# Layer A attention with the exponents stationary and a column of ones beside the values

## The chip, the cores and the metric

The kernel runs on one core of a Trainium2 chip. The metric is the device time of one launch in microseconds (us), given as the median of several runs. The core has a matrix engine (TensorE, PE in the profile; PEld are its weight loads), VectorE (DVE), ScalarE (ACT), GpSimd (POOL) and SyncE (SP), which here only issues DMAs. Sixteen DMA engines move all data between DRAM and the on-chip memory. Matmuls write to a memory called PSUM in the code.

## The reference

Four layers follow each other, A, B, A, B, each added to its input and fed by a layernorm without weights. Layer B is a linear attention over the whole sequence and is not touched by the change, apart from a step at its start that completes the output of layer A. Layer A is a recurrence over 64 segments:

```python
B, S, Dm = 1, 2048, 640;  H, Dh = 32, 192;  M, seg = 8, 32
mask = (idx[:, None] < M) | (idx[:, None] >= idx[None, :])
mem = mem0                                            # 8 rows
for s in range(64):
    h = concatenate([mem, xs], axis=1)                # 8 + 32 rows of 640
    q, k, v = h @ Wq, h @ Wk, h @ Wv                  # 32 heads of 192
    p = softmax(where(mask, q @ k.T * Dh ** -0.5, -1e9))
    o = (p @ v) @ Wo                                  # 40 rows of 640
    mem = o[:, :M];  outs.append(o[:, M:])
```

A segment needs the eight memory rows that the segment before it puts out, so the 64 segments run one after the other. All weights of layer A (Wq, Wk, Wv, Wo, 7.86 MB each in bfloat16) pass through the array in every segment.

## The kernel before

**Preparation (`A_pre`).** The last eight rows of each segment influence nothing in the recurrence. Their queries, keys and values ("tails") are made for all segments at once and stored in DRAM (`kqb_d`, `vb_d`). In the first layer this stage also lays out two of the four parts of Wo in DRAM (`lay_out_wo`, `wo_rows`), so that a later load of them has rows of 2560 bytes; the other two parts are loaded from Wo itself.

**The chain (`A_chain`).** A segment handles the other 32 rows: eight of memory, 24 of input. Its transposed rows `hT` are the stationary operand, 32 columns wide; four matmuls stand side by side in the array's four column groups (`tile_position=(0, 32 * g)`), each with 384 columns of weights moving. The 32 heads are split into four rounds of eight. For one round:

- `q_or_k` and `project` (line 988) make Q and K, 20 matmuls each; `to_raw` (line 998) copies them out on ScalarE, `to_rows` (lines 1003 to 1008) transposes them in 32x32 blocks on VectorE into `QT` and `KT`. V is projected likewise and copied into `Vp` by `v_rows` (lines 1017 and 1019).
- `next_kq` (lines 959 to 967) puts the tails of Q and K beside them and fetches the next ones, `extra_v` (line 971) fetches the tails of V. All this is on GpSimd and its DMA queue. `Vp` lies on partitions 0 to 79; its other partitions hold the input rows that `hx_transpose` (line 943) reads.
- `weigh`: `scores` puts a mask (line 1025) and six products (line 1030) into one bank, 80 keys on the partitions, 320 columns of queries; ScalarE exponentiates it into `E` (line 1085).
- `sums` (line 1099) multiplies `E` by a block of ones, so that each row of the bank holds the sums of the columns; `normalise` makes their inverse with Ln and Exp on ScalarE (lines 1104 and 1105) and VectorE multiplies `E` by it (line 1106).
- `attend` (line 1038) has the values stationary and `E` moving: eight matmuls of 80 columns. Its output is transposed as `wo_round` needs it and is copied into `OT` (lines 1044 and 1045); the tails go to `otb` (`keep_tail`, lines 1051 to 1054) and to DRAM (`store_tail`, line 1058).
- `wo_round` (line 1067), 48 matmuls of 160 columns, adds the round to the segment's output `W`. After the last round VectorE transposes the memory rows of `W` into the next `hT` (lines 1220 and 1221), which the next segment's first projection waits for, and ScalarE copies the output rows out (`keep_rows`, line 951).

The order on each engine is the program's own (`tc.manual_schedule()`), so each engine meets its instructions as they are written. `keep_busy` (line 1074) and `fill` (line 1080) issue matmuls and weight loads whose results nobody reads.

**Weights.** Not all weights fit on the chip. Three of the five pieces of Q, K and V of two rounds share slots: a slot is loaded anew in each segment (`load_slot`, line 681, on SP's queue) once the first round's projection has read it. The order of rounds turns round in every other segment. In the same way the parts 0 and 3 of Wo share `wo_end`; `load_wo` (line 698) loads the one that the last round needs, in six pieces, after `wo_round` of the first. With the tails' small transfers a segment moves 6.09 MB.

**After the chain** `post_steps` (lines 1260 and 1261, in layer B's stage) multiplies the tails' attention by Wo for 16 segments at a time; `spread_tails` orders them for it.

## Time and profile before

| | |
|---|---|
| runs | 3598.80, 3600.39, 3607.37 us; median 3600.39 |
| span of the profiled execution | 3590.5 us, 168460 instructions |
| between the span and the median | 9.9 us |
| busy in the span | PE 97%, DVE 65%, ACT 57%, POOL 44% |
| DMA | 929.38 MB, mean 259 GB/s |
| preparation, first layer | 0 to 181 us |
| chains | 181 to 1540 us and 1980 to 3340 us |
| the remainder of layer B and the second preparation | 1540 to 1980 us and 3340 to 3590 us |
| one segment of a chain | 21.0 us (median) |

The profile is one execution under the hardware profiler. Its span runs from the first to the last instruction, and the runs' times hold some work around it. "Busy" is the union of an engine's instruction times; a matmul's time holds the way through the array, so that PE can be busy all the time without being full. In lists of instructions the bracket at the end of a row tells how long the engine was idle before it and what ended that.

### The profile page before, as it was taken

How to read it: one execution, taken by the hardware profiler on the slowest of the kernel's cores; microseconds unless marked ns; L12 is line 12 of the kernel's file. 1: busy time of each engine (PE TensorE's matmuls, PEld its weight loads, DVE VectorE, ACT ScalarE, POOL GpSimd, SP SyncE). 2: the span in 40 equal slices, each digit the busy share in tenths (PEclk: the TensorE clock that was granted, in tenths of full speed). 3: DMA queues.
4: the chain of work that ended last, by engine and by line, in shares of the span. 5: the costliest groups of instructions: out<-in, count | busy, mean ns of one | idle time of the engine just before them, and what ended most of it. 6: DMA issues, size and time to landing. Idle time of an engine off the chain costs nothing.

```text
span 3590.5 us, 168460 instructions
## 1 busy us (share of the span) xinstructions
PE 3465.5 (97%) x70978; PEld 2268.6 (63%) x71399; DVE 2327.0 (65%) x6320; ACT 2032.0 (57%) x5233; POOL 1589.1 (44%) x4173
## 2 busy tenths in 40 slices
PE   9989999999999999999999899999999999999999
PEld 7756666666666666655377566666666666666553
DVE  5466666667666666746633566666666666676465
ACT  3356666666566656646432556666666666666463
POOL 3445555555555555530123455555545555555400
PEclk9999999999999999999999999999999999999999
DMA  8988888888788878860476878887888888888600
GB/s 311 334 290 288 281 295 282 278 292 299 278 284 295 289 277 278 295 224 3 146 272 217 290 275 287 290 291 278 285 294 279 290 282 292 292 281 287 222 1 30
DMA packets 452689, 929.38 MB, mean 259 GB/s; under 512 B 75338, under 2 KB 218330, under 8 KB 448858
## 3 DMA queue, kind: packets, MB, share of 16 engines
q1 hardware_dynamic: 382266, 817.56, 64.0%
q0 software_dynamic: 67744, 87.80, 7.9%
q8 instruction: 557, 9.13, 1.0%
q10 hardware_dynamic: 1920, 13.24, 0.9%
q14 instruction: 202, 1.65, 0.1%
HBM read 848.50 MB, written 73.73 MB: 257 GB/s over the span
## 4 chain that ended last, share of the span: by engine, by line
PE 55%; DMA 20%; issue 9%; DVE 7%; POOL 5%; ACT 4%; SPq 1%; PEld 0%; POOLq 0%; ACTq 0%; DVEq 0%
PE ps_qk L988 17%; DMA arena<-wo_rows 7%; DMA Vp<-vb 6%; PE ps_v L988 6%; PE ps_w L1067 6%; PE ps_pre L878 3%; PE ps_o L1038 3%; PE ps_s L1030 3%; DVE hT L943 2%; PE ps_s L1099 2%; DMA arena<-in_A_Wv_dram 2%; PE ps_s L1025 2%; PE ps_pre L902 2%; PE ps_idle L1074 2%; PE kv L1260 1%
## 5 line engine op out<-in xcount | busy, mean ns | idle before, releaser
L988 PEld LDWEIGHTS <-hT 128*32 128x32 bf16 x30720 | 746.5, 96 | 431.9 <-DVE hT L1221 27.2
L988 PE MATMUL ps_qk<-arena,hT 128*32 128x384 bf16 x20480 | 998.8, 328 | 14.6 <-DMA arena<-in_A_Wq_dram 4.2
L998 ACT ACTIVATE raw<-ps_qk 128x384 bf16<-128x384 f32 x1024 | 502.0, 490 | 383.7 <-PE ps_s L1099 250.9
L988 PE MATMUL ps_v<-arena,hT 128*32 128x384 bf16 x10240 | 534.6, 328 | 8.7 <-DMA arena<-in_A_Wv_dram 8.4
L971 POOL DMA_DIRECT2D Vp<-vb x512 | 258.4, 505 | 611.4 <-PE ps_o L1038 465.6
L1067 PE MATMUL ps_w<-arena,OT 128*32 128x160 bf16 x18432 | 446.1, 234 | 11.4 <-DMA arena<-wo_rows 10.4
L1003 DVE STREAM_TRANSPOSE KT<-raw 128x384 bf16<-128x384 bf16 x512 | 296.0, 578 | 194.5 <-ACT raw L998 190.5
L1067 PEld LDWEIGHTS <-OT 128*32 128x32 bf16 x18432 | 322.7, 96 | 103.8 <-ACT OT L1044 22.3
L1006 DVE STREAM_TRANSPOSE QT<-raw 128x256 bf16<-128x256 bf16 x512 | 227.9, 445 | 237.5 <-ACT raw L998 195.5
L959 POOL DMA_DIRECT2D kqb<-kqb x512 | 290.9, 568 | 168.9 <-POOL KT L967 147.3
L1019 DVE CAST Vp<-ps_v 64x384 bf16<-64x384 f32 x512 | 286.2, 559 | 113.6 <-ACT Vp L1017 90.0
L1106 DVE TENSOR_TENSOR E<-E,ps_s 80x320 bf16<-80x320 bf16 x512 | 247.4, 483 | 142.7 <-ACT ps_s L1105 142.3
L1058 POOL DMA_DIRECT2D otb<-otb x512 | 282.7, 552 | 128.1 <-DVE otb L1054 100.0
L1017 ACT ACTIVATE Vp<-ps_v 64x384 bf16<-64x384 f32 x512 | 246.1, 481 | 138.4 <-PE ps_v L988 122.9
L1038 PEld LDWEIGHTS <-Vp 80*128 80x128 bf16 x4096 | 189.9, 99 | 123.1 <-issue 80.5
L1038 PE MATMUL ps_o<-E,Vp 80*128 80x80 bf16 x4096 | 233.0, 201 | 31.8 <-DMA Vp<-vb 15.0
L1085 ACT ACTIVATE E<-ps_s 80x320 bf16<-80x320 f32 x512 | 221.4, 432 | 68.0 <-PE ps_s L1030 33.6
L951 ACT ACTIVATE Vp<-ps_w 32x160 bf16<-32x160 f32 x512 | 150.3, 294 | 155.1 <-DVE wt L1220 138.4
L964 POOL COPY QT<-kqb 128x64 bf16<-128x64 bf16 x512 | 124.5, 243 | 254.8 <-PE ps_s L1030 248.5
L1030 PE MATMUL ps_s<-QT,KT 128*80 128x80 bf16 (+1 forms) x3072 | 233.2, 213 | 1.6 <-POOL KT L967 1.5
L1104 ACT ACTIVATE ps_s<-ps_s 80x320 f32<-80x320 f32 x512 | 214.7, 419 | 31.2 <-PE ps_s L1099 31.2
L1030 PEld LDWEIGHTS <-KT 128*80 128x80 bf16 x3072 | 205.4, 119 | 28.7 <-issue 18.3
(156 smaller groups left out, 5446.4 us busy)
## 6 DMA issues: line engine op xcount, KB each, us to landing
arena<-wo_rows SPq DMA_DIRECT2D x780, 320.0 KB, 6.8
arena<-in_A_Wq_dram SPq DMA_DIRECT2D x427, 384.0 KB, 4.4
arena<-in_A_Wv_dram SPq DMA_DIRECT2D x427, 384.0 KB, 6.6
arena<-in_A_Wk_dram SPq DMA_DIRECT2D x768, 192.0 KB, 4.6
kqb<-kqb POOLq DMA_DIRECT2D x512, 48.0 KB, 5.1
arena<-in_A_Wk_dram SPq DMA_DIRECT2D x43, 384.0 KB, 7.8
vb<-arena POOLq DMA_DIRECT2D x128, 112.0 KB, 6.3
Vp<-vb POOLq DMA_DIRECT2D x512, 28.0 KB, 4.8
```

The costliest lines, as they stand in the source:

```text
L959: nc.gpsimd.dma_start(out=kqb[:], in_=self.kqb_d[r, :, s, :])
L971: nc.gpsimd.dma_start(out=Vs[n % 2][64:80, :], in_=self.vb_d[s, r].rearrange("g t f -> (g t) f"))
L988: nc.tensor.matmul(o[32 * g:32 * g + 32, 0:384], lhsT=hT[:, b, :], rhs=rhs, start=(i == 0), stop=(i == KC - 1), tile_position=(0, 32 * g), ...
L998: nc.scalar.activation(out=raw[:], in_=ps[:, 0:384], func=ACT.Copy)
L1003: nc.vector.transpose(out=KT[:, :, 0:64], in_=raw[:, :].rearrange("p (c j) -> p c j", j=64))
L1017: nc.scalar.activation(out=o, in_=i, func=ACT.Copy)
L1019: nc.vector.tensor_copy(out=o, in_=i)
L1030: nc.tensor.matmul(S[0:80, c0:c0 + 80 * (q1 - q0)], lhsT=KT[:, 3 * x + i, :], rhs=QT[:, x, q0:q1, :], start=False, stop=(x == 1 and i == 2 ...
L1038: nc.tensor.matmul(O[x][:, 80 * i:80 * i + 80], lhsT=Vs[n % 2][0:80, 448 * x + k:448 * x + k + 128], rhs=E[0:80, 160 * x + 80 * e:160 * x ...
L1058: nc.gpsimd.dma_start(out=self.otb_d[:, s, 96 * r:96 * r + 96], in_=otb[:, :, :].rearrange("p c t -> p (c t)"))
L1067: nc.tensor.matmul(W[32 * g:32 * g + 32, 0:160], lhsT=OT[:, c, q:q + 32], rhs=w[:, 640 * i + 160 * g:640 * i + 160 * g + 160], start=(firs ...
L1106: nc.vector.tensor_tensor(out=E[0:80, 0:320], in0=E[0:80, 0:320], in1=rc, op=ALU.mult)
```

## The change

Queries, not keys, come out on the partitions. `attend` now has `E` stationary, 32 columns of queries of one head pair at a time in one of the four column groups, and the values moving: 192 columns and one more that holds ones (`VH = 194` is the pitch). So column 192 of the output holds the softmax sum of its row. `sums`, `normalise` and the block of ones go. The output is scaled by the sum's reciprocal where it leaves PSUM (`weigh_rows`, `scaled`) and then transposed in 32x32 blocks on VectorE (`turn`). The tails of two rounds share one bank (`pair`) and are scaled, transposed and stored together. The order of the rows of Wo changes with that, so all four parts are laid out in DRAM, in 32 DMAs. The steps of a round move: `attend` follows the projection of the next K in the same turn of the loop, and the output rounds are cut and placed anew. Of the matmuls that nobody reads (`keep_busy`, 14 in a segment) one of 512 columns is left; `FILL` and `SEG_FILL` are other numbers.

```diff
-FILL = {0: 86, 2: 79}
-SEG_FILL = 2
+FILL = {0: 65, 2: 79}
+SEG_FILL = 1
+
+VH = 194
...
-        self.vb_d = dram.tile([NSEG, NR, 2, 8, 896], BF16, name=f"vb{li}")
+        self.vb_d = dram.tile([NSEG, NR, 2, 8, 4 * VH], BF16, name=f"vb{li}")
...
+                load = nc.sync.dma_start(out=tk, in_=self.wo_rows[r, :, 1280 * k:1280 * k + 1280])
...
+            self.wo_rows = dram.tile([4, P, 7680], BF16, name="wo_rows")
+
+        def lay_out_wo(r):
+            for h in range(4):
+                for G in range(2):
+                    nc.sync.dma_start(out=self.wo_rows[r, 32 * h:32 * h + 32, 3840 * G:3840 * G + 3840]
+                                      .rearrange("f (j m) -> f j m", m=640), in_=wov[8 * r + 4 * G + h])
...
-                        lay_out_wo(ri - 1)
+                        for r1 in (2 * ri - 2, 2 * ri - 1):
+                            lay_out_wo(r1)
...
-            def attend(E, n, OT=None):
-                O = [pop.tile([P, 512], F32, name=f"ps_o{x}", tag=f"o{x}") for x in range(2)]
-                for x in range(2):
-                    for k, e, i in ((0, 0, 0), (320, 1, 2), (128, 0, 1), (192, 1, 1)):
-                        nc.tensor.matmul(O[x][:, 80 * i:80 * i + 80], lhsT=Vs[n % 2][0:80, 448 * x + k:448 * x + k + 128],
-                                         rhs=E[0:80, 160 * x + 80 * e:160 * x + 80 * e + 80], start=(k == 0),
-                                         stop=(k == 192), skip_group_check=True)
-                if OT is None:
-                    OT = sp.tile([P, 6, 64], BF16, name="OT", tag="OT")
-                o = [x[:, 0:240].rearrange("p (i q) -> p i q", q=80) for x in O]
-                nc.scalar.activation(out=OT[:, 0:3, :], in_=o[0][:, :, 0:64], func=ACT.Copy)
-                nc.vector.tensor_copy(out=OT[:, 3:6, :], in_=o[1][:, :, 0:64])
-                return OT, o
-
...
+            pair = [None]
+
+            def attend(E, n):
+                O = pop.tile([P, 512], F32, name="ps_o", tag="o0")
+                V = Vs[n % 2]
+                for G in range(2):
+                    for h in range(4):
+                        nc.tensor.matmul(O[32 * h:32 * h + 32, VH * G:VH * G + 193], lhsT=E[0:80, 80 * h + 32 * G:80 * h + 32 * G + 32],
+                                         rhs=V[0:80, VH * h:VH * h + 193], start=True, stop=True, tile_position=(0, 32 * h),
+                                         skip_group_check=True)
+                if n % 2 == 0:
+                    pair[0] = pop.tile([P, 512], F32, name="ps_t", tag="o1")
+                q, m = (48, 32) if n % 2 == 0 else (64, 16)
+                for h in range(4):
+                    nc.tensor.matmul(pair[0][32 * h:32 * h + m, 0:193], lhsT=E[0:80, 80 * h + q:80 * h + q + m],
+                                     rhs=V[0:80, VH * h:VH * h + 193], start=True, stop=True, tile_position=(0, 32 * h),
+                                     skip_group_check=True)
+                return O
+
+            def weigh_rows(O):
+                rc = sp.tile([P, 2], F32, name="rc", tag="rc")
+                nc.vector.reciprocal(out=rc[:], in_=O[:, 0:2 * VH].rearrange("p (g f) -> p g f", f=VH)[:, :, 192])
+                return rc
+
+            def scaled(out, O, rc, G, eng):
+                i = O[:, VH * G:VH * G + 192]
+                if eng == "s":
+                    nc.scalar.activation(out=out, in_=i, func=ACT.Copy, scale=rc[:, G:G + 1])
                 else:
-                    nc.scalar.activation(out=otb[:, 0:3, :], in_=o[0][:, :, 64:80], func=ACT.Copy)
-                self.chain_end = [nc.vector.tensor_copy(out=otb[:, 3:6, :], in_=o[1][:, :, 64:80])]
+                    nc.vector.tensor_scalar(out=out, in0=i, scalar1=rc[:, G:G + 1], scalar2=None, op0=ALU.mult)
+
+            def keep_tail():
+                rc = sp.tile([P, 1], F32, name="rct", tag="rct")
+                nc.vector.reciprocal(out=rc[:], in_=pair[0][:, 192:193])
+                rows = sp.tile([P, 192], BF16, name="otr", tag="rawk")
+                nc.scalar.activation(out=rows[:], in_=pair[0][:, 0:192], func=ACT.Copy, scale=rc[:])
+                otb = sp.tile([P, 192], BF16, name="otb", tag="otb")
+                self.chain_end = [nc.vector.transpose(out=otb[:], in_=rows[:])]
                 return otb
 
             def store_tail(otb, s, r):
-                nc.gpsimd.dma_start(out=self.otb_d[:, s, 96 * r:96 * r + 96], in_=otb[:, :, :].rearrange("p c t -> p (c t)"))
+                nc.gpsimd.dma_start(out=self.otb_d[:, s, 192 * (r // 2):192 * (r // 2) + 192], in_=otb[:])
...
-                        nc.tensor.matmul(W[32 * g:32 * g + 32, 0:160], lhsT=OT[:, c, q:q + 32],
+                        nc.tensor.matmul(W[32 * g:32 * g + 32, 0:160], lhsT=OT[i // 6][:, i % 6 // 2, 32 * (i % 2):32 * (i % 2) + 32],
...
+            def keep_busy(ps, w):
+
+                nc.tensor.matmul(ps[0:32, 0:w], lhsT=self.ident[:, 0:32], rhs=wo_mid[:, 0:w], start=True, stop=True,
+                                 tile_position=(0, 0), skip_group_check=True)
...
-            def sums(S, E):
-                nc.tensor.matmul(S[0:80, 0:320], lhsT=ap3(self.ones_blk[0:80, :], [list(self.ones_blk[0:80, :].ap[0]), [0, 80]]), rhs=E[0:80, 0:320], start=True, stop=True,
-                                 skip_group_check=True)
-
-            def normalise(S, E):
-                rc = S[0:80, 0:320]
-                nc.scalar.activation(out=rc, in_=rc, func=ACT.Ln)
-                nc.scalar.activation(out=rc, in_=rc, func=ACT.Exp, scale=-1.0)
-                nc.vector.tensor_tensor(out=E[0:80, 0:320], in0=E[0:80, 0:320], in1=rc, op=ALU.mult)
...
+                OTs = []
+
+                def turn(n, osc):
+                    if n in (0, 2):
+                        rows = sp.tile([P, 6, 64], BF16, name="OT", tag="rawk")
+                        OTs.append([rows[:, 3 * G:3 * G + 3, :] for G in range(2)])
+                        nc.vector.transpose(out=rows[:], in_=osc[:].rearrange("p (c j) -> p c j", j=64))
+                        return
+                    if n == L:
+                        OTs.append([KT[:, 3 * G:3 * G + 3, 0:64] for G in range(2)])
+                    else:
+                        OTs.append([sp.tile([P, 3, 64], BF16, name="OT1", tag=tag)[:] for tag in ("rawk", "OTh")])
+                    for G, v in enumerate(OTs[n]):
+                        nc.vector.transpose(out=v, in_=osc[:, 192 * G:192 * G + 192].rearrange("p (c j) -> p c j", j=64))
...
                 for n in range(L):
                     raw = q_or_k("Q", n + 1)
-                    if n > 0:
-                        OT, o = attend(Ep, n - 1)
-                        tails_after(n - 1)
-                    S, E = weigh(False)
+                    if n == 1:
+                        wo_round(W, order[0], OTs[0], True, False)
+                        if s < NSEG - 1:
+                            load_wo(order[L])
+                        else:
+                            tails = [self.fetch_tails(tb, low) for tb in range(2)]
+                    elif n == 2:
+                        wo_round(W, order[1], OTs[1], False, False, range(6))
+                        otb = keep_tail()
+                    E = weigh()
                     to_rows(raw, "Q")
-                    if n > 0:
-                        otb = keep_tail(o)
                     next_kq(s, n)
-                    if n > 0:
-                        store_tail(otb, s, order[n - 1])
-                    to_rows(q_or_k("K", n + 1), "K")
-                    sums(S, E)
-                    normalise(S, E)
-                    if n == 1:
-                        wo_round(W, order[n - 1], OT, True, False)
-                        if n == 1:
-                            if s < NSEG - 1:
-                                load_wo(order[L])
-                            else:
-                                tails = [self.fetch_tails(tb, low) for tb in range(2)]
-                    if n + 1 < L:
-                        pv = v_banks()
-                        project(hT, pv, "V", n + 1, s, range(KC))
-                        v_rows(pv, n + 1)
-                    Ep = E
-                pv = v_banks()
-                OT1 = OT
-                project(hT, pv, "V", L, s, range(2))
-                wo_round(W, order[L - 2], OT1, False, False, range(6))
-                project(hT, pv, "V", L, s, range(2, KC))
-                v_rows(pv, L)
-                S, E = weigh(True)
-                OT, o = attend(Ep, L - 1, KT[:, :, 0:64])
-                tails_after(L - 1)
-                otb = keep_tail(o, True)
+                    if n == 2:
+                        store_tail(otb, s, order[1])
+                    raw = q_or_k("K", n + 1)
+                    O = attend(E, n)
+                    tails_after(n)
+                    rc = weigh_rows(O)
+                    to_rows(raw, "K")
+                    pv = v_banks()
+                    project(hT, pv, "V", n + 1, s, range(KC))
+                    osc = sp.tile([P, 384], BF16, name="osc", tag="raw")
+                    for G in range(2):
+                        scaled(osc[:, 192 * G:192 * G + 192], O, rc, G, "s")
+                    turn(n, osc)
+                    v_rows(pv, n + 1)
+                wo_round(W, order[1], OTs[1], False, False, range(6, 10))
+                E = weigh()
                 next_kq(s, L)
-                store_tail(otb, s, order[L - 1])
-                wo_round(W, order[L - 2], OT1, False, False, range(6, 8))
-                sums(S, E)
-                wo_round(W, order[L - 2], OT1, False, False, range(8, 12))
-                normalise(S, E)
+                wo_round(W, order[1], OTs[1], False, False, range(10, 12))
+                wo_round(W, order[2], OTs[2], False, False, range(6))
                 if s + 1 < NSEG:
                     hT = new_hT()
-                    hx_transpose(hT, range(1))
-                wo_round(W, order[L - 1], OT, False, False)
-                idle = pqp.tile([P, 512], F32, name="ps_idle", tag="qk")
-                keep_busy(idle, 4, 96)
-                OT, o = attend(E, L)
+                    hx_transpose(hT, range(2))
+                O = attend(E, L)
                 tails_after(L)
+                rc = weigh_rows(O)
+                osc = sp.tile([P, 384], BF16, name="osc", tag="raw")
+                scaled(osc[:, 0:192], O, rc, 0, "s")
+                scaled(osc[:, 192:384], O, rc, 1, "v")
+                turn(L, osc)
+                wo_round(W, order[2], OTs[2], False, False, range(6, 12))
                 if s == NSEG - 1:
                     self.first_tails = tails, [self.spread_tails(0, tails[0], low, "vvss")]
                 if s + 1 < NSEG:
-                    hx_transpose(hT, range(1, 4))
+                    hx_transpose(hT, range(2, 4))
                     if s + 2 < NSEG:
                         load_rows(s + 2)
-                keep_busy(idle, 5, 230)
-                wo_round(W, order[L], OT, False, True)
-                keep_busy(idle, 5, 230)
+                wo_round(W, order[L], OTs[L], False, True)
+                idle = pqp.tile([P, 512], F32, name="ps_idle", tag="qk")
+                keep_busy(idle, 512)
                 fill(SEG_FILL)
                 if s + 1 < NSEG:
                     wt = sp.tile([P, KC, 32], F32, name="wt", tag="raw")
                     for b0, b1 in ((2, 5), (0, 2)):
                         nc.vector.transpose(out=wt[:, b0:b1, :], in_=W[:, 0:160].rearrange("p (j b) -> p b j", b=KC)[:, b0:b1, :])
                         nc.vector.tensor_copy(out=hT[:, b0:b1, 0:8], in_=wt[:, b0:b1, 0:8])
-                otb = keep_tail(o)
-                store_tail(otb, s, order[L])
+                store_tail(keep_tail(), s, order[L])
                 keep_rows(W)
...
+        ow = low[:, o + 6144:o + 12288].rearrange("p (r j s x) -> p r j s x", r=4, j=6, x=16)
+        for r in range(4):
+            for b in range(2):
+                at = 192 * (r // 2) + (0 if (r + b) % 2 else 16)
+                o = ow[:, r, :, b:16:2, :]
+                i = ot[:, b:16:2, at:at + 16]
+                i = ap3(i, [list(i.ap[0]), [32, 6], *[list(d) for d in i.ap[1:]]])
+                self.ev.copy(out=o, in_=i, eng=engines[r])
...
-                lhsT = ow[:, c, :]
-                w0 = 640 * (6 * (c % 2) + c % 12 // 2)
+                G, j = c % 12 // 6, c % 6
+                lhsT = ow[:, c // 12, j, :, :].rearrange("p s x -> p (s x)")[:, G:2 * P:2]
+                w0 = 640 * (c % 12)
                 w = wo[c // 12][:, w0:w0 + 640]
```

## The prediction

> **What bounds the kernel now.** I read the page first (busy shares, the 40 slices, DMA queues), then stages, one segment of layer A's chain in stretches, its end instruction by instruction, the matmuls beside the sums, and the clock. From the page:
>
> ```profile
> PE 3465.5 (97%) x70978; PEld 2268.6 (63%) x71399; DVE 2327.0 (65%) x6320; ACT 2032.0 (57%) x5233; POOL 1589.1 (44%) x4173
> ...
> DMA  8988888888788878860476878887888888888600
> ...
> q1 hardware_dynamic: 382266, 817.56, 64.0%
> ```
>
> PE looks like the bound at 97%, but a matmul's busy time holds its latency. DMA is nearly as full in both chains (slices 3 to 17 and 23 to 37). One segment (608.76 to 629.75 us, 20.99 us) in stretches; columns: length, then PE, PEld, DVE, ACT, POOL busy, granted clock, DMA share, GB/s:
>
> ```profile
> 608.76:610.26 1.50, 1.50 (x40) 1.00 (x44) 0.38 (x3) 1.26 (x5) 0.68 (x2) 1.00 0.28 48
> 610.26:618.30 8.04, 7.89 (x173) 4.74 (x169) 6.20 (x16) 5.49 (x14) 3.33 (x12) 1.00 0.99 325
> 618.30:626.50 8.20, 8.20 (x248) 5.76 (x236) 5.54 (x15) 5.82 (x16) 4.81 (x14) 1.00 1.00 370
> 626.50:627.70 1.20, 1.20 (x30) 0.91 (x20) 0.98 (x4) 0.33 (x1) 0.91 (x3) 1.00 0.56 180
> 627.70:629.75 2.05, 1.79 (x55) 1.34 (x56) 1.58 (x6) 0.21 (x1) 1.35 (x3) 1.00 0.23 60
> ```
>
> All 16 DMA engines are full for 16.2 us on end. That is the segment's weights: nine Q, K and V pieces, whose slots come free when the first projections have read them, then six pieces of the output weights. The segment's end, in order of time:
>
> ```profile
> 627.69 0.88 PE L1067 MATMUL ps_w<-arena,OT 128*32 128x160 bf16 x40
> ...
> 628.83 0.32 PE L1067 MATMUL ps_w<-arena,OT 128*32 128x160 bf16 x8 [0.26 <-DMA arena<-wo_rows]
> ...
> 629.20 0.28 DVE L1220 STREAM_TRANSPOSE wt<-ps_w 128x96 f32<-128x96 f32 x1 [0.40 <-PE ps_w L1067]
> ...
> 629.75 0.61 PEld L988 LDWEIGHTS <-hT 128*32 128x32 bf16 x20 [0.17 <-DVE hT L1221]
> ...
> 630.14 0.33 SPq L681 DMA_DIRECT2D arena<-in_A_Wq_dram  x1
> ```
>
> The last eight matmuls wait for the sixth piece to land; then come W's transpose and hT, the next Q, and the next slot load 0.39 us after it. So a second loop closes: slot load, 18 us of transfers, last piece, W, hT, slot load. No faster attention shortens it. I worked it out for the 124 segments whose six pieces load in the usual way: counted from hT's last cast, the sixth piece lands at 19.57 us (mean and median), its matmuls start at 19.76 (median), the segment takes 21.14 (mean). In 50 of the 94 whose landing the trace tells the matmuls start within 0.1 us of the landing. The kernel is bound by its PE path and its transfers together.
>
> **The change part by part.** *The sums go.* Matmuls round one:
>
> ```profile
> 612.80 1.00 PE L988 MATMUL ps_qk<-arena,hT 128*32 128x384 bf16 x20
> ...
> 613.73 0.33 PE L1099 MATMUL ps_s<-E,ones_blk 80*80 80x320 bf16 x1
> ...
> 613.99 1.00 PE L988 MATMUL ps_v<-arena,hT 128*32 128x384 bf16 x20
> ...
> 614.81 0.99 PE L988 MATMUL ps_qk<-arena,hT 128*32 128x384 bf16 x20
> ```
>
> Projection to projection is 0.82 us with nothing between (613.99 to 614.81) and 1.19 with a sum between: 0.37 us each, four a segment, 1.48 us of PE. *Attention* was 8 matmuls of 80 columns, 0.25 us from the first to the mask that follows (615.95 to 616.20). Now 12 of 193 columns run in the projections' form, four side by side: 20 of 384 in 0.82 us is 0.107 ns a column, so 12 x 193 x 0.107 = 0.25 us. No change, except that entering it from a projection costs no change of form. *Idle matmuls* (4 of 96, 10 of 230 columns: 44.3 + 170.1 us of rows) become one of 512 on 32 columns; they only filled waits.
>
> *ACT* loses Ln (214.7 us), Exp (208.4), its share of the OT copies (125.5 + about 42) and tails (77.0), and gains 1152 scaled evictions of 192 columns, priced by the OT copy (0.327 us): 377. Net -290. *DVE* loses the multiply (247.4), OT copies (183) and tails (about 130), and gains transposes: 256 of 384 columns at 0.578 and 768 of 192 at about 0.31 (half of it, row of 128 elements 0.308), 768 reciprocals (no row; the 48-column copy's 0.203 is the ceiling, I take 0.15) and 128 scalings at 0.36: 148 + 238 + 115 + 46 = 547 against 560. *POOL* issues 256 fewer tail stores (0.552 each). All lie beside PE.
>
> *The PE path of a segment* then: 12 projections x 0.82 = 9.8; output rounds 4 x 0.84 (617.94 to 618.78) = 3.4; scores 4 x 0.65 = 2.6 (0.55 from mask to the next projection, 0.10 to change form); attention 1.0. Sum 16.8. Exposed: from the last attention its drain 0.2, reciprocal 0.2, scaling 0.4, transpose 0.35, less 0.42 of output matmuls put there, 0.75; behind the last output matmuls 0.83 as now; some 0.5 where value rows and DVE's queue (the tail's transpose ahead of QT's) hold the last two attentions. About 18.9 us against 21.0.
>
> *But the transfer loop stays*: same slots, same bytes (6.09 MB a segment), same order. Last landing 19.57, plus 0.04 to the matmul, plus 1.26 from there to the end (measured 1.22 to 1.30): 20.87 against 21.14. That is 0.27 us x 126 = **-34 us**, not the 2 us x 126 that PE sets free. What is late next is the fourth to sixth piece of the output weights, each segment.
>
> *What that wait costs.* PE now stands still some 0.75 us ahead of the last round and, in it, about 0.8 us each for the fifth and the sixth piece: over 2 us in 3.4, with no idle matmuls as cover. The trace shows what less than that does (PE alone, in order of time):
>
> ```profile
> 1318.67 0.33 PE L1025 MATMUL ps_s<-mask_st,ident 80*80 80x320 bf16 x1
> 1320.54 0.48 PE L1030 MATMUL ps_s<-QT,KT 128*80 128x80 bf16 x6 [1.54 <-POOL KT L967]
> ```
>
> and the stretch behind it (columns as above):
>
> ```profile
> 1322.00:1325.45 3.45, 3.45 (x81) 3.00 (x69) 1.42 (x5) 1.12 (x4) 2.65 (x8) 0.51 0.22 57
> ```
>
> One wait of 1.54 us, and about 1.5 us later 3.4 us are granted half the clock (0.51). At half clock the first four matmuls, which free the first slot, take 0.16 us longer (4 x 384 x 0.107): that goes into the loop. I take it in half of the segments: 0.08 x 126 = +10 (ends 0 and +38, where the last eight are slow too, 0.13 more). The other 1.7 us of PE time fit into 20.9 - 18.9. The Trainium skill, page "TensorE: Matmul & The Clock Gate", section "Why this matters for your kernels", has only idle gaps of more than about 3 us bring the half clock; by that rule gaps of 0.8 us cost nothing and the sum would be 10 us lower. Here 1.54 us was enough, so the row decides.
>
> *Small DMAs.* Value tails and kqb are fetched behind attention and scores, which now come 1 to 2 us earlier: 25 to 50 KB more fall into the full stretch, against 36 KB less (value rows 194 wide instead of 224, one tail store later). At 370 GB/s 0.1 us the one way or the other; I take +3 us (ends -12 and +45, if all the 150 KB now outside it move in).
>
> *Layout.* All four parts of the output weights are laid out in DRAM, not two: 32 issues on SP instead of 2, two more copies of 1.92 MB (19.3 us landing). The loads of parts 1 and 2 wait for them, SP's queue and the first slot loads stand behind those. DMA is idle for 10 of the 81 us from 100 to 181, and it is one prologue: +4 (ends 0 and +39). Doubled copies in spread_tails (halves of a 0.55 us and a 1.47 us copy) and strided weight columns in multiply (117 against 98 ns where this trace has stride 5, beside matmuls of 216): 0 to +5, I take 0; their cover is PE's own stream.
>
> Sum: -34 + 10 + 3 + 4 = -17 us on a span of 3590.5, to 3573.5; the median of the runs, 3600.4, lies 9.9 above the span, so **3583 us**.
>
> **The rivals.** (a) *The clock turns it slower.* One half-clock stretch hides (1.7 us lost, 2 us slack); two in a row, 3.4 us lost, do not: 18.9 + 3.4 = 22.3, 1.2 us above now. It decides where the stretch that starts in the wait is itself too idle to bring the clock back, as from 188.8 to 202.5 us, where it stayed at half for 13.7. With two in a third of the segments: (0.33 x 1.2 - 0.67 x 0.1) x 126 = +42, **3643**. Against it: a late PE waits less, so the next clock holds. (b) *The small DMAs eat the gain*: 0.3 us in the loop, **3603**, no change. For it: today's tail loads issued into the full stretch take 4.8 us to land, against 1.9 outside. (c) *The transfers get shorter*: output weights are queued 1.5 us sooner and packets land at the fast tenth, 19.07 instead of 19.57: up to 0.5 us, half of it 32 us, **3551**. Against it: the engines are at 0.99 to 1.00 already. (d) The change not doing what it says: the instruction order shows sums, Ln and Exp gone from every round, so under 0.02.
>
> **How the numbers follow.** Forecast 0.40, (a) 0.29, (b) 0.20, (c) 0.11. About 0.3%, 11 us, is what a measurement of this kernel can tell from no change. Faster: the forecast and (c) less the forecast's edge near zero, 0.49; same: (b) and that edge, 0.20; slower: (a) and the upper ends, 0.31. The range takes (c) with part of the small DMAs' lower end, 3540, up to (a) and a little of the layout's end, 3650. The forecast's own range is 3565 to 3598.
>
> **What would show it.** Right: PE's waits for the output pieces (now 10.4 us, 23 times) grow to well over 50 us in most segments; segments of 20.8 to 21.0 us; the sixth piece still near 19.6; half-clock stretches inside the chains; ACT near 1740 us busy. Wrong: segments under 20.5 us (then landings moved, and I mistook the loop), or over 21.3 with no wait for the pieces (then PE, at half clock or held by DVE, is the bound).

## The result: 4.2% slower, and the profile after

The changed kernel takes 3754.18 us (median, 3736.99 to 3781.35) against 3603.88 for the kernel before beside it: a ratio of 1.042, 95% interval 1.0366 to 1.0474. Its profiled execution took 3738.2 us, with a span of 3736.4, 145.9 over that of before. The first segment begins 11.3 us later in the span (217.1 against 205.8), and the two chains of segments are longer by 59.3 and 76.9 us; between them and behind them nearly nothing changes (0.4 and -2.1).

From the page: busy shares, granted clock and DMA share in 40 slices, two of the DMA queues.

```profile
PE 3281.7 (88%) x70850; PEld 2159.8 (58%) x71122; DVE 2357.5 (63%) x6591; ACT 1846.2 (49%) x4481; POOL 1454.6 (39%) x3917
...
PEclk9989999899999999999999899989999999999999
DMA  8887887777787877760475787777777877777600
...
q1 hardware_dynamic: 382746, 821.50, 61.8%
q8 instruction: 557, 9.13, 1.0%
```

PE went from 97% to 88% and ACT from 57% to 49%, yet DMA, which the prediction had as the bound, is less full than before (7 in 23 of the 30 slices of the chains, where 26 were 8). No engine explains the longer time by its work: the time went into waits. PEclk has slices of 8 inside the chains. Queue q8 matters below.

What TensorE waited for (us in total, times, longest):

```profile
PE ps_w L1086 <- issue: 146.8, 116, 2.2
PE ps_w L1086 <- DVE KT L1174: 125.4, 128, 1.2
PE ps_s L1033 <- DVE KT L1006: 41.8, 98, 0.5
PE ps_qk L991 <- DVE hT L1236: 39.2, 126, 0.5
...
PE ps_w L1086 <- DMA arena<-wo_rows: 6.9, 13, 3.0
```

The same two kinds of wait in before, ahead of its output rounds:

```profile
PE ps_w L1067 <- issue: 16.4, 36, 1.2
...
PE ps_w L1067 <- DMA arena<-wo_rows: 10.4, 23, 1.0
```

The waits for the output weights, forecast to grow from 10.4 us to well over 50, shrank to 6.9. Two new ones stand in front: 125.4 us for the transposed attention of the last round, and 146.8 us put down to "issue", which means that the profile shows nothing that they waited for. Before had 16.4 us of that.

One segment of usual length in stretches (998.79 to 1020.94 us, 22.15 us; columns: length, then PE, PEld, DVE, ACT, POOL busy, granted clock, DMA share, GB/s):

```profile
998.83:1000.33 1.50, 1.50 (x36) 0.88 (x32) 0.41 (x2) 1.31 (x5) 0.24 (x1) 0.85 0.19 45
1000.33:1008.33 8.00, 7.64 (x206) 4.96 (x197) 5.39 (x14) 5.05 (x12) 3.25 (x11) 1.00 1.01 353
1008.33:1015.17 6.84, 6.70 (x180) 4.62 (x173) 5.49 (x16) 4.66 (x12) 4.17 (x13) 1.00 1.03 376
1015.17:1016.82 1.65, 0.00 (x2) 0.00 (x0) 0.85 (x3) 0.15 (x1) 1.19 (x5) 1.00 0.70 248
1016.82:1018.02 1.20, 1.19 (x54) 0.99 (x53) 0.17 (x1) 0.20 (x1) 0.12 (x1) 1.00 0.26 82
1018.02:1019.03 1.01, 0.00 (x2) 0.01 (x2) 0.76 (x3) 0.22 (x1) 0.38 (x1) 1.00 0.10 27
1019.03:1020.94 1.91, 1.52 (x57) 1.17 (x62) 1.71 (x8) 0.00 (x0) 0.52 (x1) 1.00 0.07 13
```

The second and third rows are as dense as before. Then PE is idle for 1.65 us, runs 1.2, and is idle for 1.01 more. The timeline of that stretch (start, us, engine, line, operation; in brackets the idle time before it and what ended it):

```profile
1014.72 0.45 PE L1086 MATMUL ps_w<-arena,OT 128*32 128x160 bf16 x14
...
1016.82 0.52 PE L1086 MATMUL ps_w<-arena,OT 128*32 128x160 bf16 x18 [1.65 <-issue]
1017.12 0.40 PE L1044 MATMUL ps_o<-Vp,E 80*32 80x193 bf16 x8
...
1017.55 0.17 DVE L1058 RECIPROCAL rc<-ps_o 128x2 f32<-128x2 f32 x1 [1.49 <-PE ps_o L1044]
1017.82 0.42 ACT L1064 ACTIVATE osc<-ps_o,rc 128x192 bf16<-128x192 f32 x1 [2.50 <-DVE rc L1058]
1018.27 0.42 DVE L1066 TENSOR_SCALAR osc<-ps_o,rc 128x192 bf16<-128x192 f32 x1 [0.55 <-ACT osc L1064]
1018.60 0.63 DVE L1174 STREAM_TRANSPOSE KT<-osc 128x192 bf16<-128x192 bf16 x2
1019.03 1.01 PE L1086 MATMUL ps_w<-arena,KT 128*32 128x160 bf16 x48 [1.01 <-DVE KT L1174]
```

An output round stops in the middle, after 14 of 32 matmuls whose operands are all there. Behind it everything is serial: attention, reciprocal, ACT's half of the scaling, DVE's half, which waits for ACT's (both read one PSUM bank), the transposes, the last output round. The sixth piece of the output weights had landed at 1018.54.

**What the stop is.** I counted TensorE's instructions (weight loads, matmuls, waits) from hT's last cast to the next. Every segment has exactly 1024, in both kernels. Queue q8 moves one packet of 16 KB for every 256 of them (557 packets for 142,629 instructions of 64 bytes). In the whole trace TensorE stands over 0.6 us at the first instruction of such a block 123 times, and each time it goes on 1.43 us (median; 1.29 to 1.55 for eight in ten) after a q8 packet has ended; here the packet ran from 1014.43 to 1015.56, and 1016.82 is 1.26 later. So the stop is a wait for instructions. 1024 being four blocks, it falls on the same four places in every segment; the idle weight loads of `FILL` and `SEG_FILL`, which look like padding, set which four: 8, 264, 520 and 776 instructions behind the cast in before, 29, 285, 541 and 797 after. The packet that brings block 797 starts 3.7 us after block 541 has begun, in the stretch where all 16 DMA engines are full of weights, and the instructions can run 6.2 us after it has begun. Before spent 5.7 us on these 256 instructions (10.97 to 16.66 us behind the cast) and hardly noticed. After would need about 4.9 (11.09 to 16.02 in after_no_wo below, medians like the others), and stands 1.41 us a segment at 797.

In the table, "stand" is that wait at the last of the four boundaries (both that occur for after_fill193), in us a segment, counted from the start of one TensorE instruction to the start of the next, and "half clock" the time a segment at a granted clock of 0.5; segments are means over the 124 of the prediction. Kernels whose boundaries move have no one stand. A ratio is against executions of before on the same chip, whose medians lie between 3596 and 3618 us, so times of different sessions are compared by their ratios. The last three columns come from the one profiled execution, which can lie beside the median: 3738.2 us for after, 3786.9 for after_busy, 3692.72 for after_fill92, 3612.93 for split_late_tail, 3671.74 for late_tail_weigh0.

| kernel | time us | ratio to before | segment us | stand | half clock |
|---|---|---|---|---|---|
| before | 3600.39 | 1 | 21.14 | 0.22 | 0.03 |
| after | 3754.18 | 1.042 [1.0366, 1.0474] | 22.24 | 1.41 | 2.12 |
| after_drift | 3784.89 | one run | 22.57 | moves | 0.96 |
| before_drift | 3682.31 | one run | 21.82 | moves | 0.14 |
| after_fill193 | 3871.67 | 1.0767 [1.0741, 1.0792] | 23.27 | 1.26 + 1.75 | 0.20 |
| before_fill65 | 3613.07 | 1.0038 [1.0026, 1.0051] | 21.23 | 0.28 | 0.00 |
| after_fill92 | 3707.59 | 1.0244 [1.021, 1.0278] | 21.83 | 1.32 | 0.99 |
| after_fill92_split | 3651.67 | 1.0105 [1.0074, 1.0136] | 21.50 | 1.26 | 0.66 |
| after_no_wo | 3552.76 | one run | 20.72 | 0 | 0.00 |
| before_no_wo | 3538.32 | one run | 20.67 | 0 | 0.03 |
| split_late_tail | 3627.11 | 1.0082 [1.0056, 1.0108] | 21.21 | 1.04 | 0.30 |
| split_late_both | 3625.0 | 1.0076 [1.0051, 1.0101] | 21.30 | 1.08 | 0.50 |
| split_late_both53 | 3618.5 | 1.0059 [1.004, 1.0077] | 21.33 | 1.00 | 0.76 |
| late_both_no_wo | 3508.55 | one run | 20.34 | 0 | 0.00 |
| after_busy | 3754.93 | 1.0443 [1.0392, 1.0493] | 22.58 | 1.58 | 2.83 |
| late_tail_weigh | 3761.94 | 1.045 [1.0432, 1.0469] | 22.46 | moves | 0.72 |
| late_tail_weigh_busy | 3759.77 | 1.0455 [1.0431, 1.0479] | 22.40 | moves | 0.72 |
| late_tail_weigh0 | 3656.73 | 1.0159 [1.0136, 1.0182] | 21.65 | 1.40 | 0.77 |

### The profile page after: what moved, and what is told of

Its sections match the earlier page's. It is cut to its first block, busy times and chain, and to the rows that moved or that the text cites. A ratio compares the mean times of both kernels' runs of the same rounds, so it can differ in the third digit from the quotient of the medians.

```text
span 3736.4 us, 167117 instructions
## 1 busy us (share of the span) xinstructions
PE 3281.7 (88%) x70850; PEld 2159.8 (58%) x71122; DVE 2357.5 (63%) x6591; ACT 1846.2 (49%) x4481; POOL 1454.6 (39%) x3917
## 3 DMA queue, kind: packets, MB, share of 16 engines
q1 hardware_dynamic: 382746, 821.50, 61.8%
## 4 chain that ended last, share of the span: by engine, by line
PE 63%; DVE 11%; issue 9%; DMA 6%; ACT 6%; POOL 1%; ACTq 0%; SPq 0%; DVEq 0%; POOLq 0%
PE ps_qk L991 20%; PE ps_w L1086 13%; PE ps_v L991 8%; PE ps_s L1033 4%; PE ps_pre L878 3%; DMA arena<-wo_rows 3%; PE ps_s L1028 2%; PE ps_o L1044 2%; ACT Vp L954 2%; PE kv L1279 2%; PE ps_pre L905 2%; ACT osc L1064 2%; DVE KT L1006 2%; ACT raw L1001 1%; DVE osc L1066 1%
## 5 line engine op out<-in xcount | busy, mean ns | idle before, releaser
L991 PE MATMUL ps_qk<-arena,hT 128*32 128x384 bf16 x20480 | 1056.2, 339 | 52.7 <-DVE hT L1236 39.2
L991 PEld LDWEIGHTS <-hT 128*32 128x32 bf16 x30720 | 782.9, 98 | 483.5 <-issue 109.3
L1086 PE MATMUL ps_w<-arena,OT 128*32 128x160 bf16 x18432 | 500.0, 236 | 155.0 <-issue 146.8
L1086 PEld LDWEIGHTS <-OT 128*32 128x32 bf16 x18432 | 358.1, 97 | 285.0 <-issue 176.3
L1064 ACT ACTIVATE osc<-ps_o,rc 128x192 bf16<-128x192 f32 x896 | 335.3, 418 | 314.6 <-DVE rc L1058 313.1
L962 POOL DMA_DIRECT2D kqb<-kqb x512 | 291.7, 570 | 165.3 <-POOL KT L970 146.8
L1072 ACT ACTIVATE otr<-ps_t,rct 128x192 bf16<-128x192 f32 x256 | 107.8, 421 | 436.4 <-DVE rct L1070 422.7
L1022 DVE CAST Vp<-ps_v 64x384 bf16<-64x384 f32 x512 | 286.3, 559 | 35.9 <-ACT Vp L1020 20.5
L1086 PE MATMUL ps_w<-arena,KT 128*32 128x160 bf16 x6144 | 175.2, 278 | 128.3 <-DVE KT L1174 125.4
L1078 POOL DMA_DIRECT2D otb<-otb x256 | 144.5, 565 | 248.7 <-DVE otb L1074 243.1
L1086 PEld LDWEIGHTS <-KT 128*32 128x32 bf16 x6144 | 140.5, 116 | 158.0 <-DVE KT L1174 152.8
L878 PEld LDWEIGHTS <-arena 128*128 128x128 bf16 x1920 | 189.5, 99 | 43.6 <-issue 11.5
```

Source lines behind the costliest of these rows:

```text
L878: nc.tensor.matmul(ps[:, T * i:T * i + T], lhsT=w[b][:, P * c:P * c + P], rhs=xBT[:, b, :], start=(b == 0), stop=(b == KC - 1))
L962: nc.gpsimd.dma_start(out=kqb[:], in_=self.kqb_d[r, :, s, :])
L991: nc.tensor.matmul(o[32 * g:32 * g + 32, 0:384], lhsT=hT[:, b, :], rhs=rhs, start=(i == 0), stop=(i == KC - 1), tile_position=(0, 32 * g), ...
L1022: nc.vector.tensor_copy(out=o, in_=i)
L1064: nc.scalar.activation(out=out, in_=i, func=ACT.Copy, scale=rc[:, G:G + 1])
L1086: nc.tensor.matmul(W[32 * g:32 * g + 32, 0:160], lhsT=OT[i // 6][:, i % 6 // 2, 32 * (i % 2):32 * (i % 2) + 32], rhs=w[:, 640 * i + 160 * ...
```

## The experiments

**Does the stop follow the instruction count?** Two more idle weight loads in every segment make 1026 instructions, so the boundaries move by two from segment to segment.

```diff
 after_drift                    before_drift
-SEG_FILL = 1                  -SEG_FILL = 2
+SEG_FILL = 3                  +SEG_FILL = 4
```

> The changed kernel with two more weight loads that nobody reads at the end of each segment (SEG_FILL 3), so that a segment has 1026 PE instructions, not 1024, and a boundary between two blocks of 256 instructions moves on by two instructions a segment. Fetch theory (PE stands still at a block boundary because the next 256 instructions have not been fetched): a segment's time depends on where the boundary lies, from about 20.9 to 22.5 us or more, smoothly over the 126 segments, and waits without a releaser sit at the boundary wherever it is. Clock theory (idle time at the segment's end alone brings half clock) and path theory (the longer way through reciprocal, scaling and transpose): segments stay at 22.2 us all along, within 0.3.

> The kernel before with two more weight loads a segment (SEG_FILL 4), for the same drift of the boundary. Fetch theory: here too the segment's time depends on the place, 21.0 us at the place it has now and over 21.6 at some others. Clock and path theory: 21.0 to 21.2 us at all places.

The stop moved with the boundary, to instruction 781, 779, 777, 775 and so on, though the work at these places differs. The segment's length swings with it. As means of four segments in a row it goes in after from 21.3 us (boundary 3 or 41 behind the cast) to 23.9 (79), in before from 20.9 (6 or 26) to 23.2 (66). Single segments scatter widely around that; over some eleven neighbouring segments the means go from 21.6 to 23.8 and from 21.1 to 22.8. So the instruction stream can cost a segment some 2 us by its phase alone, in the old kernel too, which sits at 8, near its best.

**Two phases held still.**

```diff
 after_fill193                       before_fill65
-FILL = {0: 65, 2: 79}              -FILL = {0: 86, 2: 79}
+FILL = {0: 193, 2: 79}             +FILL = {0: 65, 2: 79}
```

> The changed kernel with FILL 193 for 65 in the first segment of the first layer: 128 more weight loads, once, which move all block boundaries of both chains by half a block. Fetch theory: the total moves by more than 40 us from 3754, either way, with the wait at another place. Clock and path theory: 3754 plus at most 10.

> The kernel before with the changed kernel's FILL, 65 for 86: block boundaries 21 instructions later in the segment, where the changed kernel has them. Fetch theory: slower than 3604 by 10 to 100 us. Clock and path theory: 3604, within 10.

after_fill193 puts boundaries at 157, 413, 669 and 925. Its waits:

```profile
PE ps_o L1044 <- issue: 189.9, 125, 3.2
PE ps_w L1086 <- DVE KT L1174: 159.3, 128, 1.4
PE ps_qk L991 <- issue: 121.2, 126, 4.0
```

Two stands a segment now (1.26 us at 413, in a projection of Q, and 1.75 at 669, in an attention) make it the slowest kernel of all, at a clock of 0.989: slow without the half clock. The other kernel is the control. Before, with its boundaries exactly where after has them, is 0.38% slower than itself and stands 0.28 us where after stands 1.41. The phase alone is not what the change did; it is the phase together with a stretch that runs its 256 instructions faster than they can be brought.

**A better phase for the changed kernel, and the shared bank.** after_fill92 has the boundaries at 2, 258, 514 and 770, beside before's 8. after_fill92_split in addition gives the last round's second half a bank of its own, and with it a reciprocal of its own, so that ACT and DVE scale side by side.

```diff
-FILL = {0: 65, 2: 79}
+FILL = {0: 92, 2: 79}
...
+                O1 = pop.tile([P, 512], F32, name="ps_o1", tag="v") if apart else O
...
-                O = attend(E, L)
+                O, O1 = attend(E, L, True)
...
-                scaled(osc[:, 192:384], O, rc, 1, "v")
+                scaled(osc[:, 192:384], O1, rc, 1, "v")
```

> The changed kernel with FILL 92 for 65: 27 weight loads more, once, which put the boundary of the instruction blocks at 2, 258, 514 and 770 instructions behind hT's cast (now at 29, 285, 541, 797); the drifting run had its shortest segments there (21.4 us). Fetch theory: most of the loss goes, 3615 to 3660. Clock and path theory: 3754 as now, at most 15 less.

> The same with the last round's second half of attention in a bank of its own (that of the projected values, free by then), so that VectorE's scaling need not wait for ScalarE's. Path theory (reciprocal, two scalings one after the other, transpose, 1.25 us of PE's wait ahead of the last output round): 0.4 us a segment, 50 us less than with FILL 92 alone. If the sixth piece of the output weights or the fetch of instructions is late instead: less than 25 us.

The phase gave 47 us (63 by the ratios), a miss: I expected 90 or more. The stand stayed (1.32 us, now at 770), since the 256 instructions ahead of it are as dense there. The split gave 56 us more, as the path theory had it; the wait that it shortens lies behind the segment's last stand. Its scaling:

```profile
662.69 0.42 ACT L1069 ACTIVATE osc<-ps_o,rc 128x192 bf16<-128x192 f32 x1 [1.83 <-DVE rc L1061]
662.72 0.42 DVE L1071 TENSOR_SCALAR osc<-ps_o,rc 128x192 bf16<-128x192 f32 x1
...
663.58 0.60 PE L1091 MATMUL ps_w<-arena,KT 128*32 128x160 bf16 x24 [0.61 <-DVE KT L1179]
```

The two scalings start 0.03 us apart instead of 0.45, and the wait ahead of the last round is 0.61 instead of 1.01 here. That chain is on the path.

**The path without the transfers.** Both kernels, without the loads of the output weights from the second segment on (the output rounds multiply by weights that were loaded earlier).

```diff
-                            load_wo(order[L])
+                            if s < 1:
+                                load_wo(order[L])
```

> The changed kernel without the loads of the last round's output weights from the second segment on (the last round multiplies with what the buffer holds; the output is another). Takes a third of the transfers out of each segment. Fetch theory: the fetch of the block that PE waits for is no longer queued behind them, its wait of 1.2 to 2.2 us falls under 0.8, segments of 19.5 to 20.5 us, 3430 to 3540 in all. Clock or path theory: the wait stays, segments over 21.2 us.

> The kernel before without the same loads (another output). My prediction's picture (PE path and transfers equally long, PE path about 20.7 us): segments of 20.5 to 20.8 us, 3540 to 3570. If the transfers alone held it: under 20 us.

With a third of q1's bytes gone (577.66 of 821.50 MB are left), after has no stand at 797 and no half clock in the segments. So the stand needs the full DMA: the fetch is late because of the weights that are moved at the same time. The packet shows it: in the first chain of after_no_wo, where the blocks begin at the same places as in after, the packet for block 797 starts 1.13 us (median) after block 541 has begun, not 3.69, and has ended 2.69 us before the block runs. (In the second chain the boundaries lie 18 instructions later, without a stand too.) But the segment is 20.72 us, and before's 20.67: my 19.5 to 20.5 was a miss, and this is the number that the prediction needed. In after_no_wo:

```profile
PE ps_w L1086 <- DVE KT L1174: 171.0, 128, 1.4
PE ps_s L1033 <- DVE KT L1006: 56.7, 126, 0.5
PE ps_qk L991 <- DVE hT L1237: 49.3, 125, 0.4
```

Gaps over 0.28 us between TensorE's instructions, counted from one start to the next, make 3.8 us a segment there: 1.59 ahead of the last output round, 0.40, 0.67 and 0.35 in the segment's first third, 0.77 behind the last output matmul. In before_no_wo they make 0.4. (Counted from a matmul's modelled end, as in the profile's lists, the 3.8 are 2.3.) The rest is 16.9 us against 20.3: the change did take 3.4 us off TensorE, 1.7 of it idle matmuls (44.3 + 170.1 us of rows over 126), and 3.4 us of waits for ACT and DVE stand in its place. Waits that idle matmuls had filled show openly, and the 1.7 us of real work turned into more of them. Nothing was left to win, even without transfers.

**Are the waits in the first third ACT's?** split_late_tail issues the tail of the last round behind the next segment's first K (shown here); split_late_both does so with the row copies (keep_rows) too, ahead of the tail; the third is split_late_both with boundaries at 41, 297, 553 and 809; the fourth is split_late_both without the loads of the output weights, as above. All stand on after_fill92_split.

```diff
                 if s > 0:
                     store_rows(s - 1)
+                    store_tail(keep_tail(), s - 1, rounds(s - 1)[L])
...
-                store_tail(keep_tail(), s, order[L])
+                if s == NSEG - 1:
+                    store_tail(keep_tail(), s, order[L])
                 keep_rows(W)
```

> Compared: the kernel after with FILL[0] 92 and the last round's second half of the attention in a PSUM bank of its own (3651.67 us, 21.50 us a segment). Edit on top of it: the tail of a segment's last round (reciprocal, ScalarE scaling otr, transpose otb, its store) is issued behind the first K transposes of the next segment, no longer ahead of the copies that close the segment; TensorE's instructions are the same. Path theory (ScalarE's 0.42 us of otr stand ahead of the row copies and of Q's and K's evictions, and TensorE waits for these 0.40 + 0.67 + 0.35 us near instructions 101, 142 and 299): these waits fall by 0.5 to 0.9 us together, the segment to 20.8 to 21.1 us, the time to 3565 to 3610 us, with the sixth piece of the output weights as the next bound (it lands 19.5 us after the last cast of hT, and 1.4 us follow). Fetch theory (the segment is held by when TensorE's instructions arrive): what is won ahead comes back as a longer stand at instruction 514 or 770, and the segment stays at 21.4 to 21.5 us, 3640 to 3655 us.

> Compared: split_late_tail. The four ScalarE row copies of the segment's outputs (keep_rows) are issued behind the next segment's first K transposes too, ahead of the tail. Path theory: the waits near instructions 101 and 142 fall to under 0.15 us each; the segment 20.8 to 21.0 us, 3560 to 3600 us, no shorter than the sixth piece allows. Rival: ScalarE's eviction of V and the exponents now stand behind this work, and the wait moves to the scores or the first attention: 21.2 to 21.5 us, 3610 to 3655 us.

> The same as split_late_both with FILL[0] 53: the blocks of 256 TensorE instructions begin at 41, 297, 553 and 809 behind the last cast of hT (in the drifting kernel 41 gave 21.31 us, 3 gave 21.36). Fetch theory: within 0.15 us of split_late_both, the stand at 809 instead of 770, 1.0 to 1.5 us. Path theory alone (the phase matters only through how far ahead the stretch is that runs dense): the same 20.8 to 21.1 us, 3560 to 3610 us.

> split_late_both without the loads of the output weights from the second segment on (the outputs use old weights). With it the kernel after had 20.72 us a segment, 3552.76 us, and the kernel before 20.67. Path theory: the waits at the start (1.4 us) and 0.4 of the wait ahead of the last output round are gone, so 19.0 to 19.5 us a segment, 3340 to 3400 us. If the slot loads of the projections' weights then end last, 20.0 to 20.6 us, 3460 to 3540 us.

The waits of split_late_tail:

```profile
PE ps_w L1091 <- issue: 104.6, 114, 2.2
PE ps_w L1091 <- DVE KT L1180: 80.2, 123, 1.0
PE ps_w L1091 <- DVE OT L1173: 51.0, 125, 0.7
...
PE ps_o L1045 <- ACT E L1108: 15.5, 98, 0.4
```

The wait of the scores for K is gone; the first attention now waits for the exponents (a 0.45 us gap) and the first output round for its transposed attention (0.72, from 0.35). The median is 25 us lower, between the two theories (40 to 85 by the path, 0 to 10 by the fetch). But before is 18.6 us faster beside it too (3598.92 against 3617.53): by the ratios, 1.0105 and 1.0082, 8 us were won, the intervals overlap, and that is the fetch theory's side. Moving the copies as well gave nothing (3625.0 against 3627.11, within the spread), as the rival had it, and the phase little (3618.5, the stand at 809 1.00, as the fetch theory had it). Without transfers the segment is 20.34, 0.38 less than after_no_wo: the time of the expectation's second case, but not for its reason, since 3.4 us of gaps for ACT and DVE are left. The same 16.9 us of work, under other waits.

**The clock by itself, and the wait ahead of the first output round.** after_busy moves the idle matmul into the wait ahead of the last output round. late_tail_weigh, on split_late_tail, issues the second round's scores ahead of the first output round, and its sister does both.

```diff
 after_busy, late_tail_weigh_busy
+                idle = pqp.tile([P, 512], F32, name="ps_idle", tag="qk")
+                keep_busy(idle, 512)
                 wo_round(W, order[L], OTs[L], False, True)
-                idle = pqp.tile([P, 512], F32, name="ps_idle", tag="qk")
-                keep_busy(idle, 512)
 late_tail_weigh, late_tail_weigh_busy
                     if n == 1:
+                        E = weigh()
                         wo_round(W, order[0], OTs[0], True, False)
...
-                    E = weigh()
+                    if n != 1:
+                        E = weigh()
```

> Compared: the kernel after (3754 us, 22.24 us a segment, 2.12 us of it at half clock). Edit: the one idle matmul of 512 columns (0.39 us at full clock) stands ahead of the last output round, where TensorE waits 1.0 to 1.25 us for the transposed attention, instead of behind it; the instructions are as many as before. Clock theory (the half clock begins where TensorE is busy too little of some 3.4 us, and it is a large part of the loss): the busy share of the stretch around the wait rises by 0.11, the half clock falls to under 1.2 us a segment, the segment to 21.6 to 21.9 us, the time to 3660 to 3715 us. Rival (the half clock is a follow-up that costs little, since the waits for instructions and for ScalarE and VectorE set the length): 22.0 to 22.3 us, 3725 to 3765 us, whatever the clock.

> Compared: split_late_tail (3627 us, 21.21 us a segment). Edit: in the second round of a segment the scores and their exponents are issued ahead of the first round's output product, which waited 0.72 us for ScalarE's two scalings and VectorE's transpose; the scores (7 matmuls, some 1.5 us) now stand in that wait. Path theory: the wait goes (0.6 to 0.7 us), the segment is 20.6 to 20.9 us unless the sixth piece (landing 19.65) holds it at 20.9: 3570 to 3600 us, level with the kernel before or up to 0.8% ahead of it. Rival (the stand for the next 256 instructions at 770, now 1.04 us, takes up what is won): 21.1 to 21.3 us, 3615 to 3635 us.

> late_tail_weigh with the idle matmul ahead of the last output round as in after_busy. Clock theory: the 0.3 us of half clock a segment that split_late_tail still had fall to under 0.1; 0.05 to 0.15 us a segment, 5 to 20 us less than late_tail_weigh. Rival: within 5 us of it.

after_busy has the same time as after and the same clock: the mean granted clock of its four executions is 0.955, that of after's four 0.952 (the 2.83 in the table belong to its slowest). So one matmul of 0.39 us in a wait of 1.2 does not hold the clock. It says nothing of what the clock costs. late_tail_weigh fell outside both theories, 135 us above split_late_tail, and says nothing on the wait: the new order gave TensorE one more instruction, 1025 a segment, so the boundaries wandered as in after_drift, and its sister's with them (3759.77, level with it, so the idle matmul gave nothing here either). One instruction taken out again:

```diff
-SEG_FILL = 1
+SEG_FILL = 0
```

> late_tail_weigh with 1024 TensorE instructions a segment again (SEG_FILL 0 in place of 1), so that the blocks stay where split_late_tail has them (3627 us, 21.21 us a segment). Path theory: without the 0.72 us wait ahead of the first output round 20.8 to 21.0 us a segment, held by the sixth piece (19.65 us) from there, 3575 to 3605 us. Fetch theory: the stand at 770 grows from 1.04 us by what is won, 21.1 to 21.3 us a segment, 3615 to 3640 us.

105 us came back for one idle weight load. It is still 30 us slower than split_late_tail; the profiled executions, 21.65 us a segment against 21.21, lie further apart than that. The 0.72 us wait is gone, but TensorE now stands 0.74 us a segment at block 514, where it stood 0.07, and 1.40 at 770 instead of 1.04. That is the fetch theory, more than in full: what is won ahead of a boundary is waited for at the boundary. Why it lost 30 us on top, part of it with 0.77 us of half clock instead of 0.30, stays open. No version that moves all the weights beat the kernel before; split_late_both53 comes nearest, 0.6% behind.

## Why the prediction was wrong

**The step that failed** is "About 18.9 us against 21.0" for the PE path, and with it "The other 1.7 us of PE time fit into 20.9 - 18.9". The work in it was right: 16.8 us were forecast, 16.9 measured, and the sum's single rows held (projection to projection 0.81 us, attention with tails 0.25). The exposed waits were not: 0.75 + 0.83 + 0.5 = 2.1 us forecast, 3.8 measured without the loads of the output weights, so that the path is 20.7 us and not 18.9. The chain behind the last attention was summed from durations, 1.15 us, of which 0.75 was to be exposed; it left out that DVE's half follows ACT's (0.45 us) and the steps between the engines: 1.59 us was exposed. And "some 0.5" for value rows and DVE's queue sat at the wrong end: 1.4 us of waits came at the segment's start, where `otr` (0.42 us on ACT) and the row copies stand ahead of the evictions of Q and K. Before issued a round's attention a round late and had no such wait; the change moved it into its own round, and I priced the operations and not the distance. A path of 20.7 us alone would still have fitted under the 20.87 of the transfer loop. But the 2 us of slack on which the forecast counted were gone, and what came on top, the fetch and the clock below, showed in full.

**The transfer loop** was read rightly and no longer mattered. The sixth piece lands at 19.50 us behind the cast (19.57 before, and forecast), so neither rival (b) nor (c) happened. But its matmuls start at 20.95, 1.45 us after it landed, for the last output round itself starts at 19.94 (19.04 before). The prediction named this case: "over 21.3 with no wait for the pieces". Both halves came true, 22.24 us and 6.9 us of waits for the pieces; the reason it gave for that case, half clock or DVE, is a part of what was found.

**The fetch of instructions** was in no rival and no row that I showed, so the sum put it at nothing, though q8 stands on the page of before. With the half clock it stands between 20.72 and 22.24. How the two divide it can be estimated from the 124 segments of after: a linear fit gives 20.64 us + 0.74 for each us of the stand + 0.26 for each us at half clock. With the means, 1.41 and 2.12, that is 20.64 + 1.05 + 0.55 = 22.24, and the constant is what after_no_wo measured by removing both (20.72). The split between stand and clock is a correlation, not an experiment (long stands and half clock often come together), and after_no_wo removes whatever else the loads cost as well.

**The half clock**, taken as +10 us (0.08 a segment, ends 0 and 38), was mis-sized: by that fit about 0.55 x 124 = 68 us. Rival (a) had the direction and the clock, but took its trigger for the wait for the pieces. In after, half clock followed within 10 us in 13 of the 15 segments with a stand over 2 us, and in 3 of the 33 with one under 1 us. A long stand alone is not enough: after_fill193 stands longer and has 0.20 us of half clock. Its stands lie further from the wait ahead of the last round; that this distance decides is not shown. Stretches of a longer case of after, columns as above:

```profile
653.60:656.28 2.68, 0.51 (x17) 0.26 (x15) 1.32 (x4) 0.43 (x1) 1.70 (x6) 1.00 0.61 211
656.28:658.48 2.20, 1.19 (x54) 0.99 (x53) 0.90 (x4) 0.42 (x1) 0.51 (x1) 0.88 0.12 31
658.48:660.30 1.82, 1.79 (x49) 1.59 (x49) 0.95 (x3) 0.00 (x0) 0.52 (x1) 0.50 0.06 14
660.30:663.50 3.20, 3.02 (x37) 1.37 (x41) 1.24 (x6) 2.04 (x6) 0.75 (x2) 0.50 0.35 92
```

A stand of 2.20 us, 1.2 us of work, a wait of 1.01; from 657.95 us, inside that wait, the clock is at half for 6.8 us. The rule weighed in the prediction (the Trainium skill, page "TensorE: Matmul & The Clock Gate", section "Why this matters for your kernels": only gaps of more than about 3 us) would have none of this; no single gap here is that long, and it was right to set the row above it.

**The small terms.** Layout of the output weights: +4 forecast; the stretch ahead of the first segment grew by 11.3, inside the ends. ACT: 1846 us against "near 1740"; the scaled evictions took 443 us (335.3 + 107.8) where 377 stood, at 0.42 us each alone instead of the copy's 0.327. DVE: 2357.5 against 2327, +30 where -13 was summed. None of these decides.

## What to carry to other kernels

Work taken off the bounding engine is won only if what it waits for gets earlier as well: write down the serial chain of the other engines for each step that is moved nearer to its consumer, with the hand-overs, before counting the freed time. In a long unrolled loop count the instructions of a turn on the bounding engine: where they make a whole number of fetch blocks, the places where blocks begin are the same in every turn, and a "wait for nothing" in the profile that moves when idle instructions are added is a wait for instructions. Hold that count and phase still when comparing two versions; one instruction more was worth 105 us here.

## What the runs showed of the hardware

TensorE's instructions come in blocks of 256 by their own DMA queue, and where after stands, under full DMA, a block runs only 6.2 us after the one before has begun: 3.7 to the start of its packet, 1.1 for the packet, 1.4 more. The first of these is not fixed: for after's block at 541, under full DMA too, it is 2.1 us, and why is not shown. The Trainium skill, page "Runtime: NRT & Kernel Launch", section "Instruction fetch mechanics", has the same 16 KiB blocks and calls the cost of crossing one mostly hidden; that held in after_no_wo (DMA 5 and 6 tenths in the chains), and in after (7 and 8) the crossing cost 1.4 us in 22. The phase of the blocks moved the segment by some 2 us with nothing changed but idle instructions (after_drift, before_drift). ACT's and DVE's reads of different columns of one PSUM bank ran one behind the other, DVE's released by the end of ACT's, 0.45 us later; on two banks they started 0.03 us apart. The release is a semaphore of the program, so these runs do not show what the bank itself would do with both at once.
